# Weight loads, GpSimd work and late tables of a Fourier-mixing and maxout kernel moved to other queues and units

## The chip, the cores and the metric

The kernel runs on one core of one Trainium2 chip. The time is device microseconds of one execution, smaller is better. The engines are named as the profile names them: PE (TensorE) does the matmuls, DVE (VectorE), ACT (ScalarE) and POOL (GpSimd) the elementwise work, and SP, ACT and POOL issue DMAs, each in the order of its own queue. DMAs from SP and ACT go through a hardware queue (q1, q10 in the profile), those from POOL through a software queue (q0), which alone can change the type on the way.

## The reference

```python
def _attn_ref(x):                      # x: (8, 3072, 256) float32
    X = np.fft.fft(x, axis=1)
    X = np.fft.fft(X, axis=2)
    return X.real.astype(np.float32)

def _moe_ref(x, w1, w2, w3, w_out):    # x: (24576, 256), w1..w3: (256, 768), w_out: (768, 256)
    h = np.maximum(np.maximum(x @ w1, x @ w2), x @ w3)
    return (h @ w_out).astype(np.float32)
```

The result of the first is reshaped to 24,576 rows and given to the second.

## The kernel before

**Mixing.** The transform along the 3072 rows is split into 24 x 128. For one batch, `Mix.s(k)` (k = 0 to 6) multiplies x, laid out once forwards and once mirrored, by 24-point matrices into `z`, and `Mix.k(q)` (q = 0 to 5) multiplies `z` by cosine and sine tables `tab` into `t`, two of 12 row groups r at a time (r = 2q + 1 and 2q + 2). `tab` has 13 groups of three parts: sine, cosine, and the sine with its sign changed (`tab_minus`). `k(q)` reads all three parts of its groups, so `k(3)` reads groups 7 and 8, `k(4)` groups 9 and 10.

**Maxout.** The transform along the 256 columns is not done on the data. It is folded into the weights: max(a, b, c) is taken as a + max(b - a, c - a, 0), so only `d2 = w2 - w1` and `d3 = w3 - w1` (`differences`, L172) pass a matrix `md` (`prep_first`, L406) to give `gE`, `gO` and `gD`; `w1` and `w_out` are folded into one linear map `gw` (`prep_second`, L426), and `twice` is a small helper row made of it. One row of the result and the mirrored row need the same products: a unit makes `gE*tE + gO*tO` for the first (`unit_plus`) and adds `gD*tO` for the second (`unit_minus`). `gD` is `gO` with another sign, -2 times, or 0 in the first row; the column `dif` holds that factor, and `sgn` the sign.

**Units.** A batch is 3 blocks of 512 columns with 6 units each, 18 units. Each unit's PSUM is read by ACT (`stmp`, L534) and DVE (`hp`, `hm`, L535); the second layer (`l2_block`, L579) adds the output of four slots per block, where POOL makes one sum per slot (`even`, L575) and issues one scattered store (L598).

**The order is written by hand.** Every engine works through its instructions in the order of the code, with semaphore waits put in for the data. `plan` (L741) hangs functions behind units: `at(0, u, fn)` calls `fn` behind unit u of batch 0. The list at L771 places the rest of the weight preparation (`prep_some`), `k(2)` to `k(5)` of batch 0, the late tables and the layout of batch 1 (`turn_chunk`, `turn_last`). `s(0)` of batch 1 comes behind unit 10.

**The beginning.** x of batch 0 comes in four parts by POOL's DMAs (L197 to L199; rows 0 to 31, 32 to 63, 64 to 95, 96 to 111, cast to bfloat16) and one by SP and ACT (rows 112 to 127). `turn_rows` and `lay_rows` (L338 to L346) lay each part out mirrored and forwards, on ACT and DVE. The six halves of w1, w2, w3 follow on POOL's queue (L201 to L208). Batch 1's x is loaded on SP in four chunks of four DMAs (`load_chunk`; the last has five small ones more); the first waits until the first half of w3 has landed (`first_half`). `turn_chunk` casts a chunk on POOL, forwards (L148) and mirrored (L151). The last chunk is cast by `turn_last`, in two halves: forwards on ACT (L159), mirrored on POOL (L161). The tile pool lets a DMA queue run eight DMAs ahead.

**POOL's list before**, after its DMAs: sign copy of groups 7 to 9 (L393), `two_row`, marks, row numbers (`store_rows`), second halves of the differences (L399), w_out (L400); then, by the plan, chunk 0, sign copy of groups 10 to 12 (in `late_tables`), chunk 1, the first sum, chunk 2, and so on.

Of the kernel before, what the change touches and what calls it, by code (L numbers as in the profile page):

```python
# [33 lines left out]
def kernel(  # L34
# [52 lines left out]
    w_late = consts.tile([128, 3 * 128], FP32, tag="w_late")  # L87
# [10 lines left out]
    def load_rows(engs, dst, b, r0, r1, after=None):  # L98
        xr = x_rows(b)
        for g in range(4):  # L100
            eng = engs[g] if isinstance(engs, tuple) else engs
            ld = eng.dma_start(out=dst[g * 24:(g + 1) * 24], in_=xr[g, :, r0:r1, :])  # L102
            if after is not None:
                tc.add_manual_dep(ld.ins, after.ins.name, AFTER, reason="weights first")

# [47 lines left out]

    def turn_last(half):

        v = turned[1, "v"]
        xs = raw[1, 3]
        d0, d1 = ((0, 17), (17, 33))[half]
        nc.scalar.copy(out=v[:, d0:d1, 96:128],  # L159
                       in_=xs[:, 0:32 * 64].rearrange("p (bb dl) -> p dl bb", dl=64)[:, d0:d1, :])  # L160
        reverse(lambda out, in_: nc.gpsimd.tensor_copy(out, in_), v[:, 33:66, :], xs, 96, 33,  # L161
                32 + d0, 32 + d1)
# [6 lines left out]
    def cols(t, jh):  # L169
        return t.rearrange("p (fc j) -> p fc j", fc=2)[:, :, jh * 384:(jh + 1) * 384]  # L170
# [73 lines left out]
    w = gen.tile([128, 10 * 128], FP32, tag="w")  # L244
    turn = 2.0 * math.pi

    def rows_of(r0, r1):
        return (w_late if r0 >= 10 else w)[:, (r0 % 10) * 128:(r0 % 10 + r1 - r0) * 128]
# [74 lines left out]
    for (m, c, own) in ((m0f, 0, 1), (m0r, 24, 3)):  # L323
        for (o0, o1, src, by) in ((0, 24, t24[:, 48 + c:72 + c], amp[:, 0:1]),
# [3 lines left out]

    tab_minus(0, 7)
    nc.vector.tensor_scalar(out=sgn, in0=pidx, scalar1=0.0, scalar2=None, op0=ALU.is_equal)  # L330
    nc.vector.tensor_scalar(out=sgn, in0=sgn, scalar1=2.0, scalar2=-1.0,
                            op0=ALU.mult, op1=ALU.add)
    nc.vector.tensor_scalar(out=dif, in0=sgn, scalar1=1.0, scalar2=None, op0=ALU.subtract)
# [10 lines left out]
    def lay_rows(copy, xs, r0, n, d0=0, d1=33):  # L344
        copy(out=xn0[:, d0:d1, r0:r0 + n],
             in_=bass.AP(xs.tensor, xs.offset + d0, [xs.ap[0], [1, d1 - d0], [64, n]]))  # L346

    def bf_rows(r0, n):
# [8 lines left out]
    tab_angles(10, 13)  # L357
    lay_rows(on_act, bf_rows(0, 32), 0, 32)
# [3 lines left out]
    dvec = gen.tile([128, 128], FP32, tag="dvec")  # L362
    nc.vector.scalar_tensor_tensor(
        out=dvec.rearrange("p (dl g) -> p dl g", g=4),
        in0=j128[:, 0:4].unsqueeze(1).to_broadcast([128, 32, 4]), scalar=64.0,
        in1=j128[:, 0:32].unsqueeze(2).to_broadcast([128, 32, 4]), op0=ALU.mult, op1=ALU.add)
    nc.vector.tensor_scalar(out=dvec[:, 2:4], in0=j128[:, 0:2], scalar1=64.0, scalar2=32.0,
                            op0=ALU.mult, op1=ALU.add)
    vm = gen.tile([128, 256], FP32, tag="vm")
    qm = gen.tile([128, 256], FP32, tag="qm")  # L370
    nc.vector.tensor_scalar(out=vm[:, 0:128], in0=dvec, scalar1=pidx, scalar2=64.0,
                            op0=ALU.mult, op1=ALU.add)
# [4 lines left out]
    turn_rows(on_act, 63, 32, 54, 65)  # L377
    turn_rows(on_dve, 63, 32, 32, 54)
    lay_rows(on_dve, bf_rows(64, 32), 64, 32)
    tab_sines(7, 10, (2,))  # L380
    tab_sines(10, 13, (0,))
# [8 lines left out]

    for ch in range(4):
        raw[1, ch] = load_chunk(1, ch, first_half)
    tab_minus(7, 10, nc.gpsimd)  # L393
# [12 lines left out]
    def prep_first(jh, bank):  # L406

        cs = slice(jh * 384, (jh + 1) * 384)
        for i, wv in enumerate((d2_bf, d3_bf)):
            for half in range(2):  # L410
                psg = bank()
                hs = slice(half * 128, (half + 1) * 128)
                for fc in range(2):
                    nc.tensor.matmul(
                        psg[:, 0:384], md[fc][:, hs],
                        wv[:, fc * DFF + jh * 384: fc * DFF + jh * 384 + 384],
                        start=(fc == 0), stop=(fc == 1))
                if half == 0:
                    nc.vector.tensor_copy(out=gE[i][:, cs], in_=psg[:, 0:384])  # L419
                else:  # L420
                    nc.scalar.copy(out=gO[i][:, cs], in_=psg[:, 0:384])
                    nc.vector.tensor_scalar(out=gD[i][:, cs], in0=gO[i][:, cs], scalar1=dif,  # L422
                                            scalar2=None, op0=ALU.mult)
                yield

    def prep_second():  # L426

        for jp in range(NJC // 2):
# [8 lines left out]
            nc.vector.tensor_copy(out=g1t[:, jp * 512:(jp + 1) * 512], in_=pst)  # L437
# [10 lines left out]
        nc.scalar.activation(out=gw[:, 514:770], in_=psw[:, 256:512], func=AX.Copy, scale=sgn)  # L448
# [3 lines left out]
        nc.vector.tensor_copy(out=twice, in_=pst[:, 0:256])  # L452
        nc.vector.tensor_scalar(out=twice[:, 0:1], in0=twice[:, 0:1], scalar1=-1.0, scalar2=None,
# [236 lines left out]
    for _ in range(35):  # L690
        nc.tensor.matmul(warm, tab[:, 0:128], tab[:, 0:512], start=True, stop=True)
    m = Mix(0)
    x0f = (lambda d: xn0[:, d, 0:128], rows_back(xr0))
    for k in range(7):
        m.s(k, x0f, pool=ps_s if k % 4 else ps_f,
            evict=nc.vector.tensor_copy if k in (1, 3) else nc.scalar.copy)
        if k == 1:
            differences(nc.vector, 0, (0,))
        if k == 2:
            nc.scalar.activation(out=md[0], in_=vm, func=AX.Sin, scale=float(-2.0 * math.pi / 256.0))  # L700
        if k == 3:
# [3 lines left out]
                                    scalar2=None, op0=ALU.mult)  # L705
            differences(nc.vector, 0, (1,))
# [60 lines left out]
    def late_tables():  # L767
        tab_sines(10, 13, (1, 2))
        tab_minus(10, 13, nc.gpsimd)
# [102 lines left out]
```

## Time and profile before

| What | us |
|---|---|
| median of 3 runs | 417.54 (416.35 to 418.46) |
| profiled execution | 417.16 |
| its span | 415.3 |
| PE busy | 397.7 (96%) |
| DVE / ACT / POOL busy | 313.1 / 266.8 / 320.4 |

The span reaches from the first to the last instruction of the program; what lies around it is 1.86 us in the profiled execution. The granted TensorE clock of the execution was 0.999 of full speed. PE's busy time by stretches of the span:

| stretch, us | PE busy, us |
|---|---|
| 15 to 20 | 3.77 of 5 |
| 20 to 30 | 8.76 of 10 |
| 30 to 50 | 18.90 of 20 |
| 50 to 55 | 3.91 of 5 |
| 55 to 60 | 5.00 of 5 |
| 60 to 120 | 59.42 of 60 |
| 120 to 400 | 280.00 of 280 |
| 400 to 415.3 | 11.84 of 15.3 |

A line of the timeline gives the start, the duration, the engine, the line of the kernel, the operation with its tiles and shapes, the count of merged instructions, and in brackets the idle time ahead of it with what ended it. A line of the waits gives who waited for whom: the sum, how many times, and the longest, in us.

### The profile page before, as it was taken

What the parts mean: (1) busy time and instruction counts of PE and PEld (TensorE: products, weight loads), DVE (VectorE), ACT (ScalarE), POOL (GpSimd) and SP (SyncE); (2) the same over time, 40 slices, a digit from 0 to 9 for tenths busy, and PEclk for the clock granted to TensorE, in tenths of its full rate; (3) what the DMA queues carried; (4) which work ended last, traced back from release to release, by engine and by line L of the source; (5) the groups of instructions that cost most, each with busy time, mean ns of one, the idle gap of its engine ahead of it and who ended that gap; (6) DMA issues with size and microseconds to landing.
All of it is one profiled execution on the core that took longest, in us unless ns stands there. A gap on an engine that the chain in (4) does not pass through costs nothing.

```text
span 415.3 us, 9110 instructions
## 1 busy us (share of the span) xinstructions
PE 397.7 (96%) x3076; PEld 269.0 (65%) x3076; DVE 313.1 (75%) x561; ACT 266.8 (64%) x488; POOL 320.4 (77%) x431
## 2 busy tenths in 40 slices
PE   1889989999999999999999999999999999999996
PEld 0455667666676677667666666666676667766665
DVE  8998766776777777687668767687678777778883
ACT  7777767666766666666775666666676666655550
POOL 9977867999988888888878788888878844445651
PEclk9999999999999999999999999999999999999999
DMA  9998895684327841396316852288312222111314
GB/s 112 165 202 176 177 230 123 153 198 109 113 76 181 199 140 65 102 218 162 104 64 165 202 112 106 88 207 179 121 52 76 66 67 76 66 65 47 108 64 140
DMA packets 130535, 52.70 MB, mean 127 GB/s; under 512 B 113073, under 2 KB 127224, under 8 KB 130488
## 3 DMA queue, kind: packets, MB, share of 16 engines
q1 hardware_dynamic: 105408, 35.93, 35.7%
q0 software_dynamic: 24144, 15.86, 16.7%
q8 instruction: 24, 0.39, 0.5%
q10 hardware_dynamic: 936, 0.33, 0.3%
q14 instruction: 23, 0.19, 0.2%
HBM read 29.02 MB, written 25.17 MB: 130 GB/s over the span
## 4 chain that ended last, share of the span: by engine, by line
PE 88%; POOL 4%; DVE 4%; issue 2%; DMA 1%; ACT 1%; POOLq 0%; DVEq 0%; ACTq 0%
PE po L545 29%; PE pse L520 14%; PE pse L528 14%; PE pse L521 14%; PE ps L476 2%; PE ps L502 2%; PE ps L474 2%; PE ps L500 2%; PE po L569 2%; PE pl L558 2%; POOL x L102 2%; DMA x<-in_x_dram 1%; DVE gD L422 1%; DMA out_dram<-ot 1%; DVE back L133 1%
## 5 line engine op out<-in xcount | busy, mean ns | idle before, releaser
L534 ACT ACTIVATE stmp<-pse 128x512 bf16<-128x512 f32 x288 | 171.3, 600 | 42.5 <-PE pse L521 29.6
L535 DVE TENSOR_TENSOR hp<-pse,stmp 128x512 bf16<-128x512 f32 x144 | 99.5, 691 | 89.0 <-ACT stmp L534 60.7
L598 POOL DMA_INDIRECT out_dram<-ot,rows_m x92 | 102.6, 1115 | 53.6 <-DVE ot L595 41.6
L520 PE MATMUL pse<-t,gE 128*128 128x512 bf16 x288 | 109.2, 379 | 2.0 <-DVE hm L535 0.7
L521 PE MATMUL pse<-t,gO 128*128 128x512 bf16 x288 | 109.0, 378 | 0.0
L535 DVE TENSOR_TENSOR hm<-pse,stmp 128x512 bf16<-128x512 f32 x144 | 99.1, 688 | 3.6 <-ACT stmp L534 3.5
L575 POOL TENSOR_TENSOR even<-even,other 128x256 f32<-128x256 f32 x92 | 66.4, 722 | 26.4 <-DVE other L572 23.3
L545 PE MATMUL po<-wout_bf,hp 128*128 128x256 bf16 x576 | 85.9, 272 | 0.0
L528 PE MATMUL pse<-t,gD 128*128 128x512 bf16 x288 | 85.6, 379 | 0.0
L545 PE MATMUL po<-wout_bf,hm 128*128 128x256 bf16 x570 | 85.3, 273 | 0.0
L545 PEld LDWEIGHTS <-hp 128*128 128x128 bf16 x576 | 56.3, 98 | 17.6 <-issue 2.4
L545 PEld LDWEIGHTS <-hm 128*128 128x128 bf16 x576 | 56.4, 98 | 16.5
L595 DVE TENSOR_TENSOR ot<-po,even 128x512 f32<-128x512 f32 x92 | 62.8, 683 | 0.3 <-POOL even L575 0.3
L148 POOL CAST x<-xs 96x544 bf16<-96x544 f32 (+2 forms) x51 | 58.6, 1155 | 4.0 <-DMA xs<-in_x_dram 4.0
L151 POOL CAST x<-xs 96x544 bf16<-96x544 f32 (+5 forms) x57 | 60.5, 1071 | 0.0
L504 ACT CAST t<-ps 128x512 bf16<-128x512 f32 x48 | 28.0, 586 | 36.1 <-PE ps L502 34.8
L481 ACT CAST z_all<-ps 128x480 bf16<-128x480 f32 x46 | 25.6, 559 | 37.8 <-PE ps L476 35.7
L528 PEld LDWEIGHTS <-gD 128*128 128x128 bf16 x288 | 27.9, 98 | 32.2
L572 DVE SCALAR_TENSOR_TENSOR other<-twice,po 128x256 f32<-128x256 f32 x92 | 43.8, 476 | 0.1
L521 PEld LDWEIGHTS <-gO 128*128 128x128 bf16 x288 | 28.1, 98 | 21.2 <-issue 2.9
L520 PEld LDWEIGHTS <-gE 128*128 128x128 bf16 x288 | 28.1, 98 | 20.2 <-DVE gE L419 1.0
L561 ACT COPY even<-pl 128x512 f32<-128x512 f32 x46 | 27.0, 588 | 9.7 <-PE pl L558 9.4
(166 smaller groups left out, 390.5 us busy)
## 6 DMA issues: line engine op xcount, KB each, us to landing
xs<-in_x_dram SPq DMA_DIRECT2D x84, 198.0 KB
out_dram<-ot SPq DMA_DIRECT2D x90, 128.0 KB
xs<-in_x_dram SPq DMA_DIRECT2D x28, 192.0 KB
raw_w<-in_moe_w_dram POOLq DMA_DIRECT2D x4, 384.0 KB
out_dram<-ot,rows_m POOLq DMA_INDIRECT x92
x<-in_x_dram POOLq DMA_DIRECT2D x12, 96.0 KB
out_dram<-ot SPq DMA_DIRECT2D x17, 64.0 KB
xs<-in_x_dram SPq DMA_DIRECT2D x32, 5.8 KB
```

The lines of the kernel that those rows point to most:

```text
L148: nc.gpsimd.tensor_copy(v[:, d0:d1, ch * 32:ch * 32 + 32], xs[:, 0:32 * 64].rearrange("p (bb dl) -> p dl bb", dl=64)[:, d0:d1, :])
L151: reverse(lambda out, in_: nc.gpsimd.tensor_copy(out, in_), v[:, 33:66, :], xs, ch * 32, 33 if ch == 3 else 32, 32 + d0, 32 + d1)
L520: nc.tensor.matmul(pse[:, 0:n], gE[i][:, js], te, start=True, stop=False)
L521: nc.tensor.matmul(pse[:, 0:n], gO[i][:, js], to, start=False, stop=True)
L528: nc.tensor.matmul(pse, gD[i][:, js], to, start=False, stop=True, skip_group_check=True)
L534: nc.scalar.activation(out=stmp[:, 0:n], in_=pses[0][:, 0:n], func=AX.Relu)
L535: nc.vector.tensor_tensor(out=dst, in0=src3, in1=stmp[:, 0:n], op=ALU.max)
L545: nc.tensor.matmul(po, hcols(jc), wout_bf[:, jc * 256:(jc + 1) * 256], start=False, stop=(jc == NJC - 1), skip_group_check=True)
L572: nc.vector.scalar_tensor_tensor(out=other, in0=twice, scalar=po[:, 256:257], in1=po[:, 0:256], op0=ALU.mult, op1=ALU.subtract)
L575: nc.gpsimd.tensor_tensor(out=line[:, 256:512], in0=line[:, 0:256], in1=other, op=ALU.add)
L595: nc.vector.tensor_tensor(out=ot, in0=po, in1=lin, op=ALU.add)
L598: stored(nc.gpsimd.indirect_dma_start(out, bass.IndirectOffsetOnAxis(ap=rows_m[0:128 - lo, b * 12 + slot: b * 12 + slot + 1], axis=0), ot[ ...
```

## The change

- **Loads.** The four halves of w2 and w3 go from POOL's queue to SP's, ahead of batch 1's chunks. The first two wait until the last of POOL's DMAs of x has landed. The chunks lose their own wait. w1 stays on POOL; its second half is issued behind a small POOL instruction (`first_op`) that waits for DVE's last copy of x.
- **First copies.** The four copies of x's third and fourth part are split differently between ACT and DVE; the angles of `md` are made earlier on DVE and its sine earlier on ACT; `sgn` and `dif` are made later.
- **Late tables.** Groups 7 to 9 keep their cosine until behind unit 0; sine, absolute value and cosine of groups 10 to 12 come behind units 2 and 3; the sign copies on POOL come behind units 1 and 3, which puts them behind `turn_chunk(1, 0)` and `turn_chunk(1, 1)` in POOL's order. `k(3)` goes from unit 3 to unit 4.
- **gD** is made from the PSUM tile instead of from `gO`. One of three copies into `g1t` and most of `twice` go from DVE to ACT; the signed copy in `gw` goes from `prep_second` to unit 20 and reads SBUF.
- **Batch 1's last chunk** is laid out behind units 7 to 9: columns 0 to 15 forwards on ACT in two pieces, 16 to 32 forwards on POOL, mirrored on POOL as before but one unit earlier.
- Four warm-up matmuls less (31 instead of 35).

```diff
+    def signed():
+        nc.scalar.activation(out=gw[:, 514:770], in_=gw[:, 256:512], func=AX.Copy, scale=sgn)
+
+    def lay_last(part):
+        d0, d1 = ((0, 8), (8, 16))[part]
+        nc.scalar.copy(out=turned[1, "v"][:, d0:d1, 96:128],
+                       in_=raw[1, 3][:, 0:32 * 64].rearrange("p (bb dl) -> p dl bb", dl=64)[:, d0:d1, :])
...
     def turn_last(half):
...
-        nc.scalar.copy(out=v[:, d0:d1, 96:128],
-                       in_=xs[:, 0:32 * 64].rearrange("p (bb dl) -> p dl bb", dl=64)[:, d0:d1, :])
+        if half:
+            nc.gpsimd.tensor_copy(v[:, 16:33, 96:128],
+                                  xs[:, 0:32 * 64].rearrange("p (bb dl) -> p dl bb", dl=64)[:, 16:33, :])
...
-    load_rows(nc.gpsimd, x0v[:, 96:112, :], 0, 96, 112)
-
-    first_half = None
+    fourth = load_rows(nc.gpsimd, x0v[:, 96:112, :], 0, 96, 112)
+
+    def load_w(eng, wdst, wsrc, jh):
+        return eng.dma_start(
+            out=cols(wdst, jh),
+            in_=wsrc.rearrange("(fc p) j -> p fc j", fc=2)[:, :, jh * 384:(jh + 1) * 384])
+
+    load_w(nc.gpsimd, w1_bf, moe_w1, 0)
     for jh in range(2):
-        for wsrc, wdst in zip((moe_w1, moe_w2, moe_w3), (w1_bf, *raw_w)):
-            wld = nc.gpsimd.dma_start(
-                out=cols(wdst, jh),
-                in_=wsrc.rearrange("(fc p) j -> p fc j", fc=2)[:, :, jh * 384:(jh + 1) * 384])
-        if jh == 0:
-            first_half = wld
+        for wsrc, wdst in zip((moe_w2, moe_w3), raw_w):
+            ld = load_w(nc.sync, wdst, wsrc, jh)
+            if jh == 0:
+                tc.add_manual_dep(ld.ins, fourth.ins.name, AFTER, reason="x first")
...
-    for (copy, a, b, c, d) in ((on_dve, 32, 54, 0, 20), (on_act, 54, 64, 20, 33)):
+    nc.vector.tensor_scalar(out=qm, in0=vm, scalar1=256.0 * ROUND, scalar2=None, op0=ALU.add)
+    nc.vector.scalar_tensor_tensor(out=vm, in0=qm, scalar=-256.0 * ROUND, in1=vm,
+                                   op0=ALU.add, op1=ALU.subtract)
+
+    nc.scalar.activation(out=md[0], in_=vm, func=AX.Sin, scale=float(-2.0 * math.pi / 256.0))
+    for (copy, a, b, c, d) in ((on_act, 54, 65, 20, 33), (on_dve, 32, 54, 0, 20)):
+        turn_rows(copy, 63, 32, a, b)
+        lay_rows(copy, bf_rows(64, 32), 64, 32, c, d)
+    for (copy, a, b, c, d) in ((on_act, 58, 64, 22, 33), (on_dve, 32, 58, 0, 22)):
         turn_rows(copy, 95, 17, a, b)
         if copy is on_act:
             turn_rows(copy, 95, 16, 64, 65)
-        lay_rows(copy, bf_rows(96, 16), 96, 16, c, d)
+        laid = lay_rows(copy, bf_rows(96, 16), 96, 16, c, d)
...
     for ch in range(4):
-        raw[1, ch] = load_chunk(1, ch, first_half)
-    tab_minus(7, 10, nc.gpsimd)
+        raw[1, ch] = load_chunk(1, ch)
+    first_op = nc.gpsimd.memset(mark, 0.0)
+    tc.add_manual_dep(first_op.ins, laid.ins.name, AFTER, reason="the two share a port")
+    load_w(nc.gpsimd, w1_bf, moe_w1, 1)
...
-                    nc.vector.tensor_scalar(out=gD[i][:, cs], in0=gO[i][:, cs], scalar1=dif,
+                    nc.vector.tensor_scalar(out=gD[i][:, cs], in0=psg[:, 0:384], scalar1=dif,
                                             scalar2=None, op0=ALU.mult)
...
-            nc.vector.tensor_copy(out=g1t[:, jp * 512:(jp + 1) * 512], in_=pst)
+            (nc.vector.tensor_copy if jp else nc.scalar.copy)(
+                out=g1t[:, jp * 512:(jp + 1) * 512], in_=pst)
...
-        nc.vector.tensor_copy(out=twice, in_=pst[:, 0:256])
+        nc.scalar.copy(out=twice[:, 1:256], in_=pst[:, 1:256])
...
-    for _ in range(35):
+    for _ in range(31):
...
-    for (u, fn) in ((0, prep_some), (0, prep_some), (1, prep_some), (1, prep_some),
-                    (2, lambda: m.k(2)), (2, late_tables), (2, prep_some), (2, prep_some),
-                    (3, lambda: m.k(3)), (3, prep_some), (4, prep_some),
-                    (5, prep_some), (5, l2_first),
+    for (u, fn) in ((0, prep_some), (0, prep_some), (0, lambda: tab_sines(7, 10, (2,))),
+                    (1, prep_some), (1, prep_some), (1, prep_some),
+                    (2, lambda: m.k(2)), (2, prep_some), (2, lambda: tab_sines(10, 13, (0,))),
+                    (3, prep_some), (3, lambda: tab_sines(10, 13, (1, 2))),
+                    (4, lambda: m.k(3)), (4, prep_some), (5, prep_some), (5, l2_first),
                     (6, lambda: m.k(4)), (7, lambda: m.k(5)), (7, m.end),
-                    (0, lambda: turn_chunk(1, 0)), (2, lambda: turn_chunk(1, 1)),
+                    (0, lambda: turn_chunk(1, 0)), (1, lambda: tab_minus(7, 10, nc.gpsimd)),
+                    (2, lambda: turn_chunk(1, 1)), (3, lambda: tab_minus(10, 13, nc.gpsimd)),
                     (5, lambda: turn_chunk(1, 2)),
-                    (8, lambda: turn_last(0)), (9, lambda: turn_last(1))):
+                    (7, lambda: turn_last(0)), (8, lambda: turn_last(1)),
+                    (8, lambda: lay_last(0)), (9, lambda: lay_last(1)), (20, signed)):
         at(0, u, fn)
```

More of the change, by code (lines that the diff above doesn't have):

```diff
@@ L327 @@
             nc.scalar.activation(out=m[:, o0:o1], in_=src, func=AX.Copy, scale=by)
+    dvec = gen.tile([128, 128], FP32, tag="dvec")
+    nc.vector.scalar_tensor_tensor(
+        out=dvec.rearrange("p (dl g) -> p dl g", g=4),
+        in0=j128[:, 0:4].unsqueeze(1).to_broadcast([128, 32, 4]), scalar=64.0,
+        in1=j128[:, 0:32].unsqueeze(2).to_broadcast([128, 32, 4]), op0=ALU.mult, op1=ALU.add)
+    nc.vector.tensor_scalar(out=dvec[:, 2:4], in0=j128[:, 0:2], scalar1=64.0, scalar2=32.0,
+                            op0=ALU.mult, op1=ALU.add)
     tab_minus(0, 7)
[L330 to L333, printed above, removed]
     back = gen.tile([96, 33 * 130], BF16, tag="back")
@@ L344, in lay_rows @@
     def lay_rows(copy, xs, r0, n, d0=0, d1=33):
-        copy(out=xn0[:, d0:d1, r0:r0 + n],
-             in_=bass.AP(xs.tensor, xs.offset + d0, [xs.ap[0], [1, d1 - d0], [64, n]]))
+        return copy(
+            out=xn0[:, d0:d1, r0:r0 + n],
+            in_=bass.AP(xs.tensor, xs.offset + d0, [xs.ap[0], [1, d1 - d0], [64, n]]))
     def bf_rows(r0, n):
@@ L357 @@
     tab_angles(10, 13)
+    vm = gen.tile([128, 256], FP32, tag="vm")
+    qm = gen.tile([128, 256], FP32, tag="qm")
+    nc.vector.tensor_scalar(out=vm[:, 0:128], in0=dvec, scalar1=pidx, scalar2=64.0,
+                            op0=ALU.mult, op1=ALU.add)
     lay_rows(on_act, bf_rows(0, 32), 0, 32)
@@ L697 @@
         if k == 1:
[L698 to L701, printed above, removed]
             halves = [t.rearrange("p (q two g) -> p two q g", two=2, g=4) for t in md]
@@ L705 @@
                                     scalar2=None, op0=ALU.mult)
+            differences(nc.vector, 0, (0,))
+        if k == 3:
             differences(nc.vector, 0, (1,))
```

36 lines of the change are left out of this document (9 added, 27 removed).

## The prediction

> **What bounds the kernel now.** I read the busy table first: TensorE (PE) is busy 397.7 of 415.3 us and the granted clock is full, so an edit counts only if it makes PE wait less. Then the waits of PE by releaser, for the stretch that the change touches:
>
> ```profile
> PE ps L474 <- DVE nat L345: 1.2, 1, 1.2
> PE ps L476 <- POOL x L161: 1.1, 1, 1.1
> PE pse L520 <- DVE hm L535: 0.7, 2, 0.4
> PE pse L520 <- DVE gE L419: 0.5, 1, 0.5
> ```
>
> All of PE's waits up to 60 us are about 4.5 us; after 60 us there are two more of 0.24 and 0.26. So everything is decided in the first 55 us, and the last gate there is batch 1's first stage, `s(0)`, which waits for GpSimd (POOL). The chain of waits shows that gate; the timeline of POOL shows what stands in front of it:
>
> ```profile
> 51.69 1.11 POOL x L161
> 52.79 0.68 POOL even L575
> 53.47 0.97 POOL x L161
> 54.44 0.05 issue
> 54.49 0.22 PE ps L476
> ```
>
> ```profile
> 19.73 1.23 POOL L272 TENSOR_SCALAR tab<-tab 128x384 bf16<-128x384 bf16 x1
> 29.58 2.00 POOL L148 CAST x<-xs 96x1056 bf16<-96x1056 f32 x1 [1.24 <-DMA xs<-in_x_dram]
> 31.54 2.08 POOL L151 CAST x<-xs 96x1056 bf16<-96x1056 f32 x1
> 33.71 1.17 POOL L272 TENSOR_SCALAR tab<-tab 128x384 bf16<-128x384 bf16 x1
> 37.62 1.99 POOL L148 CAST x<-xs 96x1056 bf16<-96x1056 f32 x1 [2.74 <-DMA xs<-in_x_dram]
> 39.55 2.00 POOL L151 CAST x<-xs 96x1056 bf16<-96x1056 f32 x1
> 42.01 0.72 POOL L575 TENSOR_TENSOR even<-even,other 128x256 f32<-128x256 f32 x1 [0.46 <-DVE other L572]
> 49.70 0.72 POOL L575 TENSOR_TENSOR even<-even,other 128x256 f32<-128x256 f32 x1 [0.90 <-ACT stmp L534]
> ```
>
> Call L0 = 29.58 and T = 37.62 the moments when chunks 0 and 1 of batch 1 have landed: POOL waits for both DMAs. From T on POOL is nearly gapless to the gate: 16.82 us (37.62 to 54.44) with only 0.46 and 0.90 us of real waiting. Where PE uses the sign copies (L272), and where it reaches the gate:
>
> ```profile
> 34.00 0.27 PE L500 MATMUL ps<-tab,z_all 128*128 128x256 bf16 x1
> 36.21 1.47 PE L442 MATMUL psw<-wout_bf,g1t 128*128 128x256 bf16 x12
> 43.11 0.27 PE L500 MATMUL ps<-tab,z_all 128*128 128x256 bf16 x1
> 53.19 0.21 PE L474 MATMUL ps<-m24f,x 96*128 96x96 bf16 x1
> ```
>
> These are `k(3)`, the product `psw`, the second half of `k(4)`, and the first matmul of the gate (the second, which needs POOL, is at 54.49).
>
> **The change part by part.**
>
> *First copies.* On VectorE (DVE) the angle work for md moves ahead and the last two parts of x are split more evenly with ScalarE (ACT). DVE copies of part 3 go from 0.90 + 1.41 us to 0.90 plus 640 elements (about 0.65 by the 1,056-element row, 1.07). Against that, 0.7 us of md rounding (0.27 + 0.42, at 19.07) comes in front. ACT gains md's sine (0.42) and about 0.8 us of copies, and loses two sines and an absolute value (0.51 to 0.61 each). I work both queues out to 18.7 us, so PE starts at about 18.85 instead of 19.29: 0.4 us earlier. With POOL's four issues gone (0.71 to 0.77 us each) the 1.41 us copy also has no reason to exceed its twin of 1.07.
>
> *gD from PSUM.*
>
> ```profile
> 23.91 1.66 DVE L422 TENSOR_SCALAR gD<-gO,dif 128x384 bf16<-128x384 bf16 x1
> 25.96 1.63 DVE L422 TENSOR_SCALAR gD<-gO,dif 128x384 bf16<-128x384 bf16 x1
> ```
>
> The same shape also took 1.24 and 0.31 us; the long ones overlap POOL's L174 (1.64 us each, at 23.82 and 25.83). Read from PSUM it is the shape of L419, 0.54 us. Bounds: 4 x 0.31 at best, no gain at worst; I take 0.54, so 4.84 - 2.16 = 2.7 us less of DVE. Together with the start, unit 0's gD matmuls move from 28.05 to about 26.4, and PE reaches the place of `psw` some 2 to 2.5 us earlier. One of the three L437 copies (0.68) and the `twice` copy (0.42) go to ACT, and `signed` (0.48) goes to unit 20: small, beside other work. Four warm-up matmuls less (0.214 each) shorten nothing: PE waits behind them.
>
> *w2, w3 on the sync queue (SP).* Four DMAs leave POOL's queue and stand on SP ahead of the 21 loads of batch 1; SP holds all of them until x's last part has landed (16.8 us by the semaphore events of the trace). Before, those loads waited for w3's first half:
>
> ```profile
> 21.64 20.73 SPq L102 DMA_DIRECT2D xs<-in_x_dram  x16
> ```
>
> When does batch 1's data then start? Early bound: SP is free after four issues of about 0.4 us, at 18.6, so 3.0 us earlier than 21.64. Late bound: each 384 KB of weights costs what two 198 KB x loads cost (0.95 us each between issues), so 4 x 1.9 from 18.2 is 25.8, while x's first packet was at 23.2: 2.6 us later. My value lies between and comes from the packet records: first data 1.0 to 1.6 us after an issue on SP, then the four loads as 1,536-byte packets of 65 ns, 64 on each of 16 engines, 4.2 us; w1's second half on POOL's queue 1.3 us; w1's first half until 18.3. That gives 23.7, against an effective 23.6 before (packets 241 by 24.0 and 857 by 25.0). The DMA engines were full either way; only the order changes. T = 37.7. The differences on DVE want w2 at 20.6 and w3 at 22.1; the same sum has them landed at about 20 and 21.5, and a miss of 1 us would be swallowed below.
>
> *POOL's new order, the part that decides.* w1's second half waits for the last DVE copy (18.7, was issued at 17.02); behind it stand the memsets, row numbers, both differences and w_out, which then goes out at about 26 instead of 27.42. The sign copies go **behind** the chunk casts: rows 7 to 9 behind chunk 0, rows 10 to 12 behind chunk 1. PE needs the first for `k(3)` (moved from unit 3 to 4) and the second for `k(4)`'s second half. First copy done: L0 + 4.13 + 1.17. w_out held batch 1's loads up for about 2 us (two issues at 29.5 and 32.9 took 3.4 and 2.4 us); going out earlier it now falls into chunk 0, so L0 is 29.6 to 31.6, say 31. `k(3)` can start at 36.3, where PE wants it at about 33.5. Second copy: T + 3.93 + 1.17 = 42.8, against 43.11 before. So nearly all of the front's gain is gone at `k(4)`.
>
> *The gate.* From T: casts 3.93, sign copy 1.17, add 0.67, casts of chunk 2 4.01, add and gap 0.90, scatter 1.2, first mirrored half 1.12, add and gap 0.88, scatter 1.05, the new forward half (544 elements, 1.09 by L148's 96x544 rows), second mirrored half 1.0: 17.0 us, against 16.82. That is +1.17 + 1.09 for two pieces, -0.72 for the add that now falls behind the gate, -1.36 for the two waits, which vanish because DVE is no later. PE stands at the gate at 54.7 instead of 54.49.
>
> **Sum.** Front -2.5 at `psw`, given back at `k(3)` and `k(4)` (+2.2), rest of it lost in the wait at the gate; gate +0.2 from POOL, +0.1 from T. Behind the gate PE has no gap to win. Span 415.6, or 417.5 with the 1.86 us around it (417.16 - 415.3). The median of the runs is 417.54, 0.4 above the profiled execution, so on their scale 417.8.
>
> **Rivals.**
> - *Chunks land early, the front survives in part.* For it: SP queues the loads from 18.6 on, and DMA throughput is uneven from 16 to 18 us. Against: all 16 engines share the bytes, and 24.2 us was the end of w before. Every us that T comes earlier moves both copies and the gate by 1 us, down to T = 34.6: 414.9. 0.5% needs T under 35.5.
> - *Slower: `k(3)` becomes the bound.* Place: the sign copy behind chunk 0. If w_out and w1 push L0 beyond 32, `k(3)` starts after 37.3 and PE reaches the gate later than POOL; from there each us of L0 costs 1 us. L0 = 34, or all loads later by 2.6 us: 420 to 420.5. For it: POOL's waits for DMA are already the longest (1.24, 2.74). Against: 1.3 us of cover at the gate.
> - *It does not do what it says*: gD stays slow or w2 and w3 come late on SP. With the gate at POOL this changes nothing below 2 us: 417.8 again, counted with the forecast.
> - *PE's clock drops while it waits for `k(3)`.* In the timeline the weight loads of the first eight warm-up matmuls start 0.43 us apart, later ones 0.214, so a cold stretch costs about 7 x 0.21 = 1.5 us; the wait is 2.8 us in my sum, the longest gap seen after warm-up is 1.2. The gate covers half: 418.7. The Trainium skill, "TensorE: Matmul & The Clock Gate", section "HAM oscillation", puts the limit at an idle gap of about 3.4 us; no run here shows it, and by it the wait stays just short.
>
> **How the numbers follow.** Forecast 0.50 (own range 416.9 to 418.9), early chunks 0.22, late `k(3)` 0.22, clock 0.06. About 0.5% (2.1 us) is what a measurement can tell from no change. Of early chunks 0.16 passes it, of late `k(3)` 0.18, of the clock 0.02: faster 0.16, same 0.64, slower 0.20. The range takes in both bounds of T but for their outer ends: 415.1 to 420.2.
>
> **What would show it.** gD near 0.54 us and PE at the gD matmuls before 27 us; a new PE wait on POOL's sign copy before `k(3)` of 1 us or more and a smaller one in `k(4)`; the gate at 54 to 55.5; chunk 1 cast from 37 to 38.5. Wrong if the first mirrored matmul of batch 1 comes before 53, or if no wait on the sign copy appears.

## The result and the profile after

The changed kernel takes **418.61 us** (median of 20 runs, 417.32 to 420.61) against 416.75 us of the kernel before (20 runs, 416.08 to 418.46, taken beside it): ratio **1.0042, interval 1.003 to 1.0053**, about 1.75 us slower. That is clear of the noise, though less than the 0.5% that the prediction took for the least that could be told. The profiled execution took 418.9 us with a span of 417.1 (before 417.16 and 415.3); the granted clock was 0.995 instead of 0.999.

First the waits of PE in the profile after, for 15 to 60 us (who waited for whom: sum, times, longest, us):

```profile
PE psg L430 <- POOL d_bf L184: 1.6, 1, 1.6
PE psg L430 <- DVE d_bf L184: 1.6, 1, 1.6
PE ps L492 <- POOL x L171: 0.8, 1, 0.8
PE ps L490 <- DVE sgn L401: 0.4, 1, 0.4
```

Before, the front had no wait for the weights' differences (`d_bf`); now there are two of 1.6 us. The wait at the gate (L492, the second matmul of batch 1's `s(0)`) is still there. GpSimd's timeline shows what stands ahead of the gate:

```profile
18.77 0.72 POOL L212 DMA_DIRECT2D w_bf<-in_moe_w_dram  x1 [0.15 <-issue]
...
28.02 3.23 POOL L184 TENSOR_TENSOR d_bf<-raw_w,w_bf 128x768 bf16<-128x768 f32 x2 [6.34 <-DMA w_bf<-in_moe_w_dram]
31.20 0.92 POOL L416 DMA_DIRECT2D wout_bf<-in_moe_w_out_dram  x1
32.16 2.00 POOL L149 CAST x<-xs 96x1056 bf16<-96x1056 f32 x1
34.11 2.05 POOL L152 CAST x<-xs 96x1056 bf16<-96x1056 f32 x1
36.26 1.19 POOL L286 TENSOR_SCALAR tab<-tab 128x384 bf16<-128x384 bf16 x1
39.35 1.99 POOL L149 CAST x<-xs 96x1056 bf16<-96x1056 f32 x1 [1.91 <-DMA xs<-in_x_dram]
```

The second half of w1 is issued at 18.77, and GpSimd waits 6.34 us for it, until 28.02. Chunk 0 is no longer waited for; chunk 1 is, until T = 39.35 (before 37.62). PE's timeline, at the first gD matmul, at `k(3)`, at `psw` and at the gate:

```profile
31.22 0.59 PE L544 MATMUL pse<-t,gD 128*128 128x512 bf16 x2
38.71 0.27 PE L516 MATMUL ps<-tab,z_all 128*128 128x256 bf16 x1
39.14 1.47 PE L459 MATMUL psw<-wout_bf,g1t 128*128 128x256 bf16 x12
56.35 0.22 PE L492 MATMUL ps<-m24r,x 96*128 96x96 bf16 x1 [0.78 <-POOL x L171]
```

The gD matmuls come 3.2 us later than before (28.05), `psw` 2.9 us later (36.21), the gate 1.86 us later (54.49). From the gate to the end of the span there are 360.75 us, before 360.8: the whole difference was made ahead of it. Without GpSimd PE would have reached the gate at 56.35 - 0.78 = 55.57, so **two paths arrive nearly together, and both are over a microsecond later than before**: the front (weights, differences, PE) and GpSimd's chain from T.

The weights' lateness is seen on DVE (idle time ahead in brackets), and in the last column of the stretches behind 18 us, which is what the DMA engines moved (GB/s); the first window is of the kernel before, the other three of the kernel after:

```profile
22.09 0.96 DVE L184 TENSOR_TENSOR d_bf<-raw_w,w_bf 128x768 bf16<-128x768 f32 x1 [1.56 <-DMA raw_w<-in_moe_w_dram]
```

```profile
18.00:20.00 2.00, 0.77 (x18) 0.74 (x18) 1.77 (x5) 0.28 (x2) 1.97 (x4) 1.00 0.97 322
```

```profile
18.00:20.00 2.00, 1.59 (x34) 1.42 (x34) 1.18 (x6) 0.98 (x3) 1.26 (x5) 1.00 0.85 118
19.00:20.00 1.00, 1.00 (x28) 1.00 (x26) 0.34 (x1) 0.56 (x1) 0.94 (x4) 1.00 0.64 72
20.00:21.00 1.00, 1.00 (x29) 1.00 (x26) 0.53 (x3) 0.62 (x2) 0.71 (x5) 1.00 0.87 312
```

x's last part landed at 17.44; SP, which had waited for it, issued w2 at 17.46. By the packet records the first packet of w2 ended at 18.97, 1.5 us later, but few followed: the engines moved 72 GB/s from 19 to 20 us and 312 only behind 20. (The expectation of e9 below has the first packets at about 19.9; that is where their flow sets in.) From 18 to 20 us that makes 118 GB/s, where before, with w already queued behind x on GpSimd's queue, it was 322.

### The profile page after: what moved, and what is told of

The parts are those of the page before. It is cut to its first block, busy times and chain, and to the rows that moved or that the text cites. A ratio compares the mean times of both kernels' runs of the same rounds, so it can differ in the third digit from the quotient of the medians.

```text
span 417.1 us, 9108 instructions
## 1 busy us (share of the span) xinstructions
PE 399.0 (96%) x3072; PEld 269.5 (65%) x3072; DVE 309.3 (74%) x559; ACT 267.1 (64%) x491; POOL 318.2 (76%) x429
## 3 DMA queue, kind: packets, MB, share of 16 engines
q1 hardware_dynamic: 106496, 37.50, 36.9%
## 4 chain that ended last, share of the span: by engine, by line
PE 76%; POOL 11%; SPq 5%; DMA 5%; issue 2%; DVE 0%; POOLq 0%
PE po L561 26%; PE pse L536 12%; PE pse L544 12%; PE pse L537 12%; SPq L102 4%; DMA xs<-in_x_dram 4%; POOL x L102 3%; PE po L585 2%; POOL x L152 2%; PE pl L574 2%; PE ps L492 2%; PE ps L490 2%; POOL x L149 2%; PE ps L518 2%; PE ps L516 2%
```

## The experiments

Each kernel is the changed kernel with the edit shown, unless it says otherwise, and was timed in five rounds beside the kernel before. T is where GpSimd begins chunk 1 of batch 1, the gate is the first mirrored matmul of batch 1; both are from one profiled execution each. "Pieces" are what the change put on GpSimd behind T: the second sign copy (1.17 us) and the forward half of the last chunk (1.14 us; 1.09 had been worked out).

| kernel | pieces behind T | T | gate | gate - T | PE's wait there | span | ratio, interval |
|---|---|---|---|---|---|---|---|
| before | none | 37.62 | 54.49 | 16.87 | 1.09 | 415.3 | 1 |
| after | both | 39.35 | 56.35 | 17.00 | 0.78 | 417.1 | 1.0042, 1.003 to 1.0053 |
| e1 loads back | both | 38.89 | 55.91 | 17.02 | 1.56 | 416.9 | 1.0023, 1.0008 to 1.0038 |
| e2 pieces back | none | 37.89, no wait | 56.16 | PE last | 0 | 416.9 | 1.0034, 1.0021 to 1.0047 |
| e3 both back | none | 37.14 | 51.97 | 14.83 | 0.17 | 413.0 | 0.9976, 0.9958 to 0.9994 |
| e4 before + gD | none | 37.50 | 53.67 | 16.17 | 1.10 | 414.8 | 0.9992, 0.9979 to 1.0005 |
| e5 e3 + forward half | one | 38.37 | 54.21 | 15.84 | 2.17 | 415.2 | 0.9996, 0.9981 to 1.0012 |
| e6 e3 + sign copies | one | 37.97 | 53.90 | 15.93 | 0.52 | 415.1 | 0.9991, 0.9975 to 1.0006 |
| e7 e2 + w1 early | none | 40.66 | 55.46 | 14.80 | 0.94 | 416.2 | 1.0004, 0.9991 to 1.0017 |
| e8 after + one piece | three | 39.07 | 57.13 | 18.06 | 1.94 | 419.6 | 1.0053, 1.0034 to 1.0071 |
| e9 earlier release | both | 36.78, no wait | 55.95 | GpSimd waited 2.09 ahead of its first sum | 0.26 | 416.7 | 1.0018, 1.0003 to 1.0034 |
| e10 e7 + earlier release | none | 37.44 | 55.00 | PE last | 0 | 416.0 | 0.9931, 0.9906 to 0.9955 |
| e11 w1 early | both | 38.98 | 56.06 | 17.08 | 0.62 | 416.8 | 1.0047, 1.003 to 1.0065 |
| e12 e7 + w2 released early | none | 37.31 | 52.47 | PE last | 0 | 413.4 | 0.9966, 0.9952 to 0.998 |

### e1: the loads as before

```diff
-    load_w(nc.gpsimd, w1_bf, moe_w1, 0)
+    first_half = None
     for jh in range(2):
-        for wsrc, wdst in zip((moe_w2, moe_w3), raw_w):
-            ld = load_w(nc.sync, wdst, wsrc, jh)
+        for wsrc, wdst in zip((moe_w1, moe_w2, moe_w3), (w1_bf, *raw_w)):
+            wld = load_w(nc.gpsimd, wdst, wsrc, jh)
...
-        raw[1, ch] = load_chunk(1, ch)
-    first_op = nc.gpsimd.memset(mark, 0.0)
...
-    load_w(nc.gpsimd, w1_bf, moe_w1, 1)
+        raw[1, ch] = load_chunk(1, ch, first_half)
```

> The changed kernel with the loads as before: all six halves of w1, w2, w3 on GpSimd's queue behind x, no wait for the last copy, batch 1's loads waiting for w3's first half. All else stays changed. Theory (batch 1's second chunk lands late, and the gate s(0) follows it by 17.0 us): chunk 1 is cast from 37.6 instead of 39.35, the gate opens at 54.6 instead of 56.35, the span falls by 1.7 us to 415.4, level with before. Rival A (the waits of the front, 1.6 us twice and TensorE at half clock, set the time): they go, and the span falls by 3 us or more. Rival B (GpSimd's two added pieces set it): the span stays at 417.

Measured 1.0023, span 416.9. PE's waits in its profile:

```profile
PE ps L513 <- POOL tab L286: 2.0, 2, 1.1
PE ps L489 <- POOL x L171: 1.6, 1, 1.6
```

The front is back (first gD matmuls at 27.80), and the waits of 1.6 us for the differences have shrunk to 1.2 in sum. At once the waits on the sign copies appear that the prediction had expected, in `k(3)` (0.86 us) and `k(4)` (1.12 us), and the gate stands at T + 17.02. T itself, at 38.89, came back by only 0.5 us in this execution, where the theory wanted 37.6. So the time of before did not come back; the span is the one that rival B (GpSimd's added pieces) had named. The interval of 1.0008 to 1.0038 overlaps that of the changed kernel.

### e2: GpSimd's pieces as before

```diff
-        d0, d1 = ((0, 8), (8, 16))[part]
+        d0, d1 = ((0, 17), (17, 33))[part]
...
-        if half:
-            nc.gpsimd.tensor_copy(v[:, 16:33, 96:128], ...)
...
+    tab_minus(7, 10, nc.gpsimd)
     nc.gpsimd.memset(two_row, 0.0)
...
-                    (0, lambda: turn_chunk(1, 0)), (1, lambda: tab_minus(7, 10, nc.gpsimd)),
-                    (2, lambda: turn_chunk(1, 1)), (3, lambda: tab_minus(10, 13, nc.gpsimd)),
+                    (0, lambda: turn_chunk(1, 0)), (2, lambda: tab_minus(10, 13, nc.gpsimd)),
+                    (2, lambda: turn_chunk(1, 1)),
```

> The changed kernel with GpSimd's work as before: sign copy of groups 7 to 9 ahead of the memsets, that of 10 to 12 ahead of chunk 1, the last chunk forwards on ScalarE alone. The loads stay changed. Theory: chunk 1 still lands at 39.35; from there 17.0 less 1.17 and 1.09, so GpSimd would be ready at 54.1, but TensorE itself comes to the gate at about 55.6 (it waited 0.8 for 56.35), so the span falls by 0.8 us only. Rival A (front): no change. Rival B (added pieces): it falls by 1.8 us, to the time of before.

Measured 1.0034, span 416.9: next to nothing. The wait at the gate is gone, and PE's waits are all in the front:

```profile
PE psg L428 <- POOL d_bf L181: 2.7, 1, 2.7
PE psg L428 <- DVE d_bf L181: 0.8, 1, 0.8
```

GpSimd now follows PE: in its timeline the first sum waits 2.77 us for DVE. With the pieces gone, the late weights set the time by themselves, as rival A had it: PE came to the gate at 56.16, not at 55.6. The theory that T alone decides fell here.

### e3: both

> Both edits at once: loads and GpSimd's work as before; gD from PSUM, the new split of the first copies and the other moves stay. Theory: chunk 1 at 37.6, GpSimd ready at 52.4, TensorE at the gate at 51 to 52, so the gate opens at 52.4 and the span is 413.2, 2 us less than before. Rival A: as e1. Rival B: as e2, no better than before.

The edits of e1 and e2 together. Measured 0.9976 (0.9958 to 0.9994), 1 us under the kernel before. The profiled execution, span 413.0, is one of the two shortest of its twelve. What is left of PE's waits up to 60 us:

```profile
PE ps L485 <- DVE sgn L398: 0.7, 1, 0.7
PE psg L425 <- DVE d_bf L181: 0.5, 1, 0.5
PE ps L487 <- POOL x L168: 0.2, 1, 0.2
```

Undoing one part alone won 0.19% or 0.08%, neither of them clear of the noise; undoing both won 0.66%, which is. So the two costs lie **side by side**, and each covers most of the other. What remains of the change here (first copies, gD, the late sines, copies moved to ACT) is a small gain.

### e4: gD alone

```diff
-                    nc.vector.tensor_scalar(out=gD[i][:, cs], in0=gO[i][:, cs], scalar1=dif,
+                    nc.vector.tensor_scalar(out=gD[i][:, cs], in0=psg[:, 0:384], scalar1=dif,
```

(on the kernel before)

> The kernel before with one line changed: gD is made from the PSUM tile. Theory: VectorE's gD falls from 4.84 us in sum to about 2.4 and unit 0's gD matmuls come 1 to 1.5 us earlier, but the gate stays at 54.4, so the time stays within 0.1 per cent of before. Rival A (front): 1 us faster or more.

Measured 0.9992 (0.9979 to 1.0005). `psw` came at 35.40 instead of 36.21, and PE waited 1.10 us at the gate as before. The gate did not stay at 54.4, as the theory had it: it came at 53.67, since GpSimd had waited less for DVE and ACT and was as much earlier. In the ratio those 0.8 us would be 0.9981; the interval takes in that and no change.

### e5 and e6: the two pieces apart

Both have the loads as before. e5 puts only the sign copies back, so the forward half stays behind T; e6 puts only the forward half back.

> The changed kernel with the loads as before AND the two sign copies where they were (before chunk 0, and early behind unit 2), but the forward half of batch 1's last chunk still on GpSimd. Both parts undone gave a chain of about 14.7 us from the landing of chunk 1 (T) to the gate and a span of 413.0; one piece of 1.09 us more makes it 15.8. Theory (the two GpSimd pieces add up behind T, each worth its own length): no PE wait on a sign copy, gate at T + 15.8, that is about 53 at T = 37.1, PE waits there about 1.2 us, span about 414.0, ratio to before 0.996 to 0.999. Rival (the sign copies are the whole cost, the forward half is covered): span 413.0, ratio 0.9976 as with both undone.

> The changed kernel with the loads as before AND the last chunk's forward copy wholly on ACT, but the two sign copies still behind the chunk casts. Theory: gate at T + 15.9, and PE waits on the sign copies in k(3) and k(4), 2.0 us in sum as in the run with the loads alone undone; the wait at the gate then falls below 0.5 us; span 414.5 to 416, ratio 0.999 to 1.003. Rival (the forward half is the whole cost, the sign copies are covered): span 413.0, ratio 0.9976.

The start of chunk 1 and the gate, first of e5, then of e6:

```profile
38.37 2.00 POOL L149 CAST x<-xs 96x1056 bf16<-96x1056 f32 x1 [2.82 <-DMA xs<-in_x_dram]
```

```profile
54.21 0.22 PE L490 MATMUL ps<-m24r,x 96*128 96x96 bf16 x1 [2.17 <-POOL x L171]
```

```profile
37.97 1.99 POOL L149 CAST x<-xs 96x1056 bf16<-96x1056 f32 x1 [2.02 <-DMA xs<-in_x_dram]
```

```profile
53.90 0.22 PE L486 MATMUL ps<-m24r,x 96*128 96x96 bf16 x1 [0.52 <-POOL x L168]
```

The distances are 15.84 and 15.93, where 15.8 and 15.9 had been expected: 14.83 and one piece more. The ratios are 0.9996 and 0.9991. The rivals, that one of the two pieces is covered, wanted 0.9976 in e5 and e6; e5's interval leaves that out, e6's (from 0.9975) does not. What speaks in e6 are its distance and two waits of 0.35 and 0.36 us on the sign copies. T lay 0.8 to 1.3 us later than hoped for in both, and e5's ratio missed its range (0.996 to 0.999). The two waits in e6 came to 0.7 us, not to the expected 2.0.

### e7: w1's second half let go

```diff
     load_w(nc.gpsimd, w1_bf, moe_w1, 0)
+    load_w(nc.gpsimd, w1_bf, moe_w1, 1)
...
     tc.add_manual_dep(first_op.ins, laid.ins.name, AFTER, reason="the two share a port")
-    load_w(nc.gpsimd, w1_bf, moe_w1, 1)
```

(on top of e2)

> The changed kernel with GpSimd's pieces where they were before (this alone gave 418.68, PE waited 2.7 us for GpSimd's difference and 0.8 us for DVE's), and w1's second half issued directly behind its first half instead of behind DVE's last copy of x; w2 and w3 stay on the SP queue. It tells which part of the loads is the cost. If it is the hold on w1's second half: it lands by about 24 instead of 28, the wait of 2.7 us goes, and the span falls by 2 to 2.7 us to about 414.5, ratio about 0.998. If it is w2 and w3 on the SP queue: w1's second half lands early, but the differences then wait for w2 and w3, PE still waits 2 to 3 us in the front, and the ratio stays at 1.002 to 1.004.

Measured 1.0004, between the two expectations, and between e2 (1.0034) and e3 (0.9976), 0.30 and 0.28% from them. So the hold on w1's second half and the place of w2 and w3 cost about the same, 1.2 us each. Not all of the second is the front: in the profile GpSimd opened the gate, behind the latest T of all (40.66). The waits:

```profile
PE psg L428 <- DVE d_bf L181: 2.6, 1, 2.6
PE ps L490 <- POOL x L168: 0.9, 1, 0.9
```

The wait for w1 is gone and that for w2's first half has grown from 0.8 to 2.6: w1's second half is now among the transfers that go ahead of it.

### e8: a dose more on GpSimd

```diff
+    spare = consts.tile([128, 3, 128], BF16, tag="spare")
...
                     (2, lambda: turn_chunk(1, 1)), (3, lambda: tab_minus(10, 13, nc.gpsimd)),
+                    (3, lambda: nc.gpsimd.tensor_scalar(out=spare, in0=tabs[:, 10:13, 0, :], scalar1=-1.0,
+                                                        scalar2=None, op0=ALU.mult)),
```

> The changed kernel, and one GpSimd instruction of the size of a sign copy (128x384, about 1.17 us) more behind the second sign copy, its result read by nobody: a dose of the suspected cost, between T and the gate. If the chain from T to the gate sets the time of the changed kernel: gate at T + 18.2, PE waits there about 2 us instead of 0.8, span 417.1 + 1.2 = 418.3, ratio to before about 1.007, by T's own scatter of a microsecond more or less. If the late front sets it: span at most 0.4 us more, ratio 1.004 to 1.005.

In the profile the gate moved as the chain says (18.06 against 17.00) and PE waited 1.94 us. The ratio, 1.0053, is only 0.0011 above that of the changed kernel, less than the 0.0028 of a whole dose and near what the rival (the late front) had named, 1.004 to 1.005; the intervals overlap, and over all runs this experiment does not decide. The profiled execution is the longest of its seven, and its span of 419.6 has more in it than the dose: 362.5 us behind the gate instead of 360.8. The stretches behind the gate tell why (the third column from the right is the granted clock):

```profile
56.00:57.00 1.00, 0.00 (x0) 0.00 (x0) 0.00 (x0) 0.00 (x0) 1.00 (x2) 1.00 1.01 175
57.00:58.00 1.00, 0.87 (x10) 0.68 (x11) 0.00 (x0) 0.11 (x1) 0.93 (x3) 0.68 0.95 234
58.00:59.00 1.00, 1.00 (x4) 0.38 (x3) 0.00 (x0) 0.71 (x2) 0.90 (x1) 0.50 0.91 235
59.00:60.00 1.00, 1.00 (x4) 0.38 (x3) 0.33 (x1) 0.34 (x1) 0.18 (x2) 0.50 1.03 250
60.00:61.00 1.00, 1.00 (x6) 0.62 (x5) 0.71 (x2) 0.60 (x1) 0.00 (x0) 0.61 0.99 192
```

After the wait PE ran some 3.4 us at half clock, which makes up those 1.7 us. Behind the gate nothing covers that.

### e9: w2 and w3 released by x's third part

```diff
-    for r0 in (0, 32, 64):
-        load_rows(nc.gpsimd, x0v[:, r0:r0 + 32, :], 0, r0, r0 + 32)
+        third = load_rows(nc.gpsimd, x0v[:, r0:r0 + 32, :], 0, r0, r0 + 32)
...
-                tc.add_manual_dep(ld.ins, fourth.ins.name, AFTER, reason="x first")
+                tc.add_manual_dep(ld.ins, third.ins.name, AFTER, reason="x first")
```

> The changed kernel with one difference: w2 and w3 on the SP queue wait for the last DMA of x's third part (rows 64 to 95) instead of the fourth, so that SP may issue them while the last part is still under way. In the changed kernel they were issued at 17.46 us, their first packets ended at about 19.9, and from 17.5 to 20 us the DMA queues moved only some 100 GB/s. Theory (that hold is what makes weights and chunks late): issue at about 15.5, w2's first half landed near 20 instead of 22.0, PE's wait for DVE's difference (1.6 us) gone, chunk 1 landed (T) 1 to 1.9 us earlier, at 37.5 to 38.4, gate at T + 17.0 = 54.5 to 55.4, span 415.3 to 416.1, ratio to before 1.000 to 1.002. Rival (the DMA engines, not the hold, set it: x's last part is pushed back and nothing is won): x's last part lands 1 us later, PE starts later, T within 0.5 of 39.35, ratio 1.004 or more.

Both sides were partly right. The start of PE and of chunk 1:

```profile
20.60 0.24 PE L490 MATMUL ps<-m24f,nat 96*128 96x96 bf16 x1 [2.17 <-DVE sgn L401]
```

```profile
36.78 2.00 POOL L149 CAST x<-xs 96x1056 bf16<-96x1056 f32 x1
```

SP issued at 14.93; chunk 1 was there before GpSimd came to it (36.78, 2.6 us earlier than in the changed kernel), and PE has no wait for a difference any more. But x's last part lost what the weights won: PE starts at 20.60 instead of 18.62, and then runs at half clock (third column from the right):

```profile
20.00:25.00 5.00, 4.40 (x56) 4.43 (x57) 3.42 (x11) 1.72 (x5) 3.16 (x11) 0.56 1.16 266
25.00:30.00 5.00, 4.87 (x34) 3.17 (x34) 2.85 (x5) 3.49 (x9) 2.61 (x2) 0.75 0.65 128
```

So the first gD matmuls came at 31.34, no earlier than in the changed kernel (31.22). The ratio of 1.0018 is inside what the theory expected; the gate (55.95) and the span are above it. The hold behind x's last part is thus a cause of the late T, and letting go of it has a price of 2 us at the start and, in this execution, some 7 us at half clock.

### e10 and e12: released early, GpSimd's pieces undone

e10 is e7 with the release of e9. e12 lets only w2's first half go by the third part:

```diff
-                tc.add_manual_dep(ld.ins, fourth.ins.name, AFTER, reason="x first")
+                tc.add_manual_dep(ld.ins, (third if wdst is raw_w[0] else fourth).ins.name, AFTER,
+                                  reason="x first")
```

> GpSimd's pieces where they were before, w1's second half directly behind its first, and w2 and w3 on SP released by x's third part instead of the fourth. With the hold by the fourth part this kernel gave 1.0004 (T at 40.66, PE waited 2.6 us for DVE's difference, gate = T + 14.8). Theory: the wait of 2.6 us falls below 1, T at 38 to 39, gate at 53 to 54, span 414 to 415, ratio 0.9975 to 0.9995, about that of the version with both parts undone (0.9976). Rival (the SP queue itself costs it, by its order or its share of the engines, whenever the loads are let go): the wait on the difference stays at 2 us or more, ratio 1.000 or more.

> GpSimd's pieces where they were before, w1's second half directly behind its first, and only w2's first half released by x's third part; w3's first half waits for the fourth part, and the second halves stand behind it on SP. With both released by the third part the profiled run had PE's start at 21.69 us instead of 18.6 (x's last part 3 us late) and still no wait on a difference; the runs spread from 413.39 to 417.76 and gave 0.9931. Theory (between x's third and fourth part the DMA engines have room for some of the weights, not for all): PE starts at 18.6 to 20, PE's wait for DVE's difference below 1 us (2.6 us where both wait for the fourth part), gate at 53 to 54.5, span 413.5 to 415.5, ratio 0.992 to 0.998. Rival (x's last part is pushed back by as much as the weights win): start at 20.5 or later, ratio 0.998 to 1.002. Other rival (w3 and the second halves are what is late): the wait on a difference stays above 2 us, ratio 1.000 or more.

e10 gave 0.9931 (0.9906 to 0.9955), faster than either side had expected, in six runs that lie far apart (413.39 to 417.76, the profiled one the longest). e12 gave 0.9966 (0.9952 to 0.998). The starts, first of e10, then of e12, and e12's gate:

```profile
21.69 0.20 PE L488 MATMUL ps<-m24f,nat 96*128 96x96 bf16 x1 [3.75 <-DVE sgn L399]
```

```profile
20.40 0.20 PE L489 MATMUL ps<-m24f,nat 96*128 96x96 bf16 x1 [2.44 <-DVE sgn L400]
```

```profile
52.47 0.20 PE L491 MATMUL ps<-m24r,x 96*128 96x96 bf16 x1
```

Beside e7, which differs from it in this release alone, e12 starts PE 1.9 us later (20.40 against 18.45, and later than the theory's 18.6 to 20) and has the gate 3.0 us earlier, without a wait between: 2 us given at the start are cheap where they save the waits for the weights. The clock stayed at 1.00 here, unlike in e9 after a like wait; how much of the gain is that was not separated. Of e10 the one profile, its longest run, shows a start at 21.69 and half clock from 23 to about 26. Its five shorter runs have a mean clock of 1.0 where this one has 0.995, so they had no such stretch; when PE started in them was not seen. e3, e10 and e12 are faster than both kernels; e12's interval is the narrower of the two best.

### e11: w1's second half let go, nothing else

> The changed kernel, with w1's second half issued directly behind its first half and nothing else changed; the sign copies and the forward half stay on GpSimd behind the chunk casts. With GpSimd's pieces undone this step moved the gD matmuls of the first unit from 31.95 to 30.14 us but chunk 1's landing T from about 38 to 40.66. Theory (gate = T + 17.0, whatever the front does): the front is 1 to 2 us earlier and nothing of it is won; at T = 39.4 to 40.7 the gate is at 56.4 to 57.7, PE waits there 2 to 3 us, span 417 to 418.5, ratio 1.003 to 1.007. Rival (the late front sets it): span 415 to 416, ratio 0.999 to 1.002.

Measured 1.0047, as the theory had it, and the gate at T + 17.08. But its premise failed: the front came no earlier (gD matmuls at 31.09 against 31.22), since the 1.6 us on DVE's difference grew to 3.6. So this run does not separate the two theories; without its hold w1's second half went ahead, and w2's first half came later (DVE's first difference at 23.81 instead of 22.09).

## Why the prediction was right, and where its steps were not

The forecast of 417.8 stood beside a median of 417.54, a ratio of 1.0006; measured is 1.0042, 1.5 us more. The time was near and the form of the sum held; most of the way to it did not, and part of the agreement is luck: at the gate two misses hid each other (PE comes there 2.2 us later than before, GpSimd 1.9, and the gate is 1.86 us later, not 4). Of the signs that the prediction had named only gD's time came. PE was at the gD matmuls at 31.22 (before 27), chunk 1 was cast from 39.35 (37 to 38.5), the gate was at 56.35 (54 to 55.5), and the wait on the sign copy, whose absence was to show it wrong, was absent.

- **Gate = T + 17.0.** Shown: 17.00, and 17.02 and 17.08 in the two other kernels with the same work on GpSimd; each piece moves it by its own length in the profiles (14.8, 15.8 and 15.9, 17.0, 18.1).
- **Nothing to win behind the gate.** 360.75 against 360.8 us: held.
- **T = 37.7 is the term that was mis-sized**: 39.35, 1.65 us more, as much as the gate is late. With T as forecast the late front would still have brought PE to the gate at 55.57 instead of 54.7, so either alone makes half of the miss or more. The step that failed is "The DMA engines were full either way; only the order changes". The issue was at 17.46 instead of 16.8, as x's last part landed later. "First data 1.0 to 1.6 us after an issue" held (1.5), but behind it the flow was thin until 20. The packet counts of batch 1 that the prediction had put at an effective 23.6 before and 23.7 after (241 by 24.0, 857 by 25.0) came at 25.42 and 26.22, so 1.2 to 1.4 us later and not 0.1. Then two loads of chunk 0 took SP 3.72 and 4.04 us to issue (20.13 and 23.89), and from 27 to 29 us the DMA engines were nearly empty, a share of 0.21 and 0.20; what held SP up there was not tried. T also scatters: 37.14 to 38.89 in the six kernels with the loads on GpSimd, 38.98 to 40.66 in four with w2 and w3 held on SP, and at most 37.89 in e2. How much of the 1.65 us is that scatter stays open.
- **The landings of the weights** were the second wrong step ("about 20 and 21.5, and a miss of 1 us would be swallowed below"). w2's first half came at 22.0, not at 20, and w1's second half, which the sum gave 1.3 us on GpSimd's queue, took from 18.77 to 27.95. So w_out went out at 31.20 instead of about 26: its packets run from 32.98 to 37.27, among those of chunk 1 and not of chunk 0, and what that cost T was not tried. The gain of 2.5 us at `psw` became a loss of 2.9. In the profile PE still comes to the gate 0.78 us ahead of GpSimd, so the miss was swallowed there, as forecast; e2 shows that it is the next bound, not far below.
- **The wait for `k(3)`**, which was to be 1 us or more, did not come: PE was so late (38.71) that the sign copy had been done for a microsecond (37.45). By the prediction's own words that step was wrong. Chunk 0 was cast from 32.16, just past the 32 from which the rival "late `k(3)`" was to count, but `k(3)` was not held up by the sign copy, so that rival is not what made the kernel slower. e1 shows that only its cover was misjudged: with the loads as before `k(3)` waits 0.86 us and starts at 36.22, where 36.3 had been worked out.
- **First copies and gD.** PE started at 18.62 (18.85 forecast) and gD took 0.61 to 0.62 us (0.54): sizes right, and worth nothing at the gate of the changed kernel, as said (alone, in e4, gD goes with a gate 0.8 us earlier).
- **The clock** did drop, but elsewhere: at 23.5 us, after the wait for w2, not at `k(3)`. The stretches of the changed kernel, with the granted clock third and the GB/s last from the right:

```profile
22.00:23.00 1.00, 0.00 (x0) 0.00 (x0) 0.91 (x2) 0.25 (x2) 0.00 (x0) 1.00 1.04 378
23.00:24.00 1.00, 0.89 (x5) 0.52 (x6) 1.00 (x3) 0.00 (x0) 0.00 (x0) 0.79 1.14 300
24.00:25.00 1.00, 1.00 (x7) 0.74 (x6) 1.00 (x3) 0.48 (x1) 0.00 (x0) 0.50 1.20 265
...
27.00:28.00 1.00, 1.00 (x5) 0.27 (x4) 0.41 (x2) 0.75 (x2) 0.00 (x0) 1.00 0.21 37
28.00:29.00 1.00, 0.08 (x1) 0.00 (x0) 0.93 (x2) 0.33 (x1) 0.98 (x1) 1.00 0.20 46
```

PE works at 0.50 for some 3.5 us here and then stands idle until 29.71 for GpSimd's difference. At full clock it would have stood idle longer, so in this execution the cost is covered at least in part. The 20 runs do not show it covered throughout: 13 have a mean clock of 0.995 or 0.996 and a median of 418.90, seven have 0.999 or 1.0 and a median of 418.25. So the drop is in most runs and goes with 0.65 us; whether the clock makes the time or a longer wait makes both was not separated. The seven at full clock are still 1.5 us above the kernel before.

## What to carry to other kernels

Two late paths that meet at one gate hide each other: undoing one part alone moved little (0.08 and 0.19%), both together 0.66%, so undo parts in pairs before calling one harmless. A load that is moved to another queue and held until an earlier one has landed pays for the gap behind that landing, here 1.5 us to its first packet and 2.5 us until the DMA engines moved 300 GB/s; released one transfer earlier, all of it (0.9931) or a part (0.9966), it was faster than held (1.0004), though PE then started 2 to 3 us later. Work put behind a DMA wait on the engine that opens the gate adds its full length, however idle that engine is elsewhere; where another path comes last, as in e2, taking it away wins nothing.

## What was not expected of the hardware

**A load on the software queue started late.** From 20 to 24 us of the changed kernel (packets, MB, share of the engines), with w2, w3 and batch 1 on SP's queue and w1's second half on GpSimd's:

```profile
q1 hardware_dynamic: 904, 1.32, 91.2%
q0 software_dynamic: 94, 0.07, 11.7%
```

The load on GpSimd's queue, issued at 18.77, got 94 packets beside 904, and all 94 behind 22.8: its first packet started at 22.86, 4.1 us after the issue, where w1's first half and w_out took 1.8 us (15.36 to 17.14, 31.20 to 32.98). The Trainium skill, "DMA: Bandwidth & Descriptors", section "Queues, rings and completion order", says that each DMA engine takes turns between the queues that have work for it, packet by packet. Once both had packets the trace agrees with that: from 24 to 25 us there are 133 of the software queue and 149 of the hardware queue. What held the first packet back, the descriptors or something else, is not shown.

**The clock drops after short waits, and not after each.** In the changed kernel 1.60 us of waiting at 21.5 was followed by half clock; in e8 1.94 us at the gate was; in e5 2.17 us at the same gate was not (clock 1.00 throughout from 50 to 60 us). Ahead of PE's start 2.17 us in e9 was, 2.44 us in e12 was not (1.00 from 17 to 27 us). The Trainium skill, "TensorE: Matmul & The Clock Gate", section "HAM oscillation — how this bites in real kernels", gives idle gaps over about 3.4 us as the limit. Here gaps well below it were enough, so a wait of 1.6 to 2.2 us must be counted as one that may cost half a clock for 3 to 7 us more.
